# The second mixing's first layer by one level of Strassen's seven products

## The chip, the core and the metric

One core of one Trainium2 chip runs the whole program. The metric is device time in microseconds, the median of the runs shown; the profile is one further execution of the same program. PE is the matrix engine, DVE the vector engine, ACT the scalar engine, POOL the GpSimd engine, SP the engine that issues most DMAs.

## What is computed

```python
def _moe2_ref(x, g_ln, w_ch1, w_ch2):
    mu = np.mean(x, axis=-1, keepdims=True)
    var = np.mean((x - mu) ** 2, axis=-1, keepdims=True)
    xn = (x - mu) / np.sqrt(var + 1e-06) * g_ln
    ch = np.maximum(xn @ w_ch1, 0.0) @ w_ch2
    return x + ch
```

This is the last of three parts. Before it stand a linear attention (8 batches, 8 heads, 576 positions of 64) and a first mixing of tokens and channels (hidden sizes 256 and 1536). The second mixing, above, works on 8 x 576 = 4608 tokens of 512 channels with 2048 hidden channels. The weights arrive as 64-bit floats.

## The kernel before

**Numbers.** Each fp32 operand of a matmul is split into two parts, hi and lo, and each product is three matmuls (`PASSES`, hi-hi, hi-lo, lo-hi). A 64-bit weight is decoded by `decode` (L92): a rescale, three bit operations (L113, L120, L126) and a split (ACT copies hi, POOL subtracts for lo).

**First stage.** `Phase1` (L676) runs nine blocks of 512 tokens. A step is one hidden slice `f` of 128: `L1` (L695; its matmuls L704) makes 12 matmuls of 512 columns into a PSUM tile of the pool `ps_hid`, which has two buffers; ACT and DVE (`relu_split`, L148) turn it into a tile `h`; `L2` (L711; L721) adds 12 matmuls into four accumulators, two steps later (`LAG`). Every block has 12 steps. Beside it run attention and the weight decode, hung into the steps by `later` (so many ticks ahead; a step has four ticks) and by `loads.pump` (so many operations after each layer). `finish` writes the block to DRAM, `y_store` (L651) turns it by four transposes per 128 tokens.

**Second stage.** `Norm` (L802) brings a block back from DRAM and normalises it: DVE subtracts the mean, POOL scales, ACT and DVE split into `xT`. `Phase2` (L850) runs the nine blocks, with 16 steps each. A step is `L1` (L858; matmuls L865; weights `wa2`, moving operand `xT`), the relu and split, and `L2` (L872; matmuls L880; weights `h`, moving operand `wb2`), 12 matmuls of 512 columns each. That makes 9 x 16 x 12 = 1728 matmuls per layer. A `g` stands for two steps: tiles `wa2[g]` and `wb2[g]` lie in the pool `main`, except those of `g` 0 and 1 (steps 0 to 3 of each block), which lie in the pool `w2pool`, further up in SBUF; `xT` and `h` lie in `main`.

**What sets the order.** The program is written out by hand: each engine takes its instructions strictly in the order in which the code issues them, each waiting for semaphores. So an ACT copy that waits for a DMA holds up every ACT instruction behind it. SP's DMAs are issued in order too. The main loop (L999) issues L1, relu and split, decode work, L2 of two steps before, decode work.

**The memories.** PSUM: four accumulators (`ps_acc`), two tiles for L1 (`ps_hid`), two for everything else (`ps_att`). In SBUF the tag `w` of `main` has twelve tiles of 8 KB per partition, for the weights of both stages in turn; the tag `s` has two staging tiles.

## Time and profile before

| | |
|---|---|
| median of 3 runs | 1650.42 us (1649.99 to 1651.19) |
| span of the profiled execution | 1648.4 us, 2.0 us under the median |
| PE busy | 98% of the span |
| DVE, ACT, POOL busy | 40%, 25%, 23% |
| mean granted clock of PE | 0.998 of full speed |
| DMA | 119.71 MB, mean 73 GB/s |

A matmul's duration in the profile is modelled and longer than its slot on the engine, because matmuls are pipelined. The pace is read from start to start: the first of a group of twelve to the first of the next group.

### The profile page before, as it was taken

What the parts mean: (1) busy time and instruction counts of PE and PEld (TensorE: products, weight loads), DVE (VectorE), ACT (ScalarE), POOL (GpSimd) and SP (SyncE); (2) the same over time, 40 slices, a digit from 0 to 9 for tenths busy, and PEclk for the clock granted to TensorE, in tenths of its full rate; (3) what the DMA queues carried; (4) which work ended last, traced back from release to release, by engine and by line L of the source; (5) the groups of instructions that cost most, each with busy time, mean ns of one, the idle gap of its engine ahead of it and who ended that gap; (6) DMA issues with size and microseconds to landing.
All of it is one profiled execution on the core that took longest, in us unless ns stands there. A gap on an engine that the chain in (4) does not pass through costs nothing.

```text
span 1648.4 us, 19985 instructions
## 1 busy us (share of the span) xinstructions
PE 1619.5 (98%) x7954; PEld 1360.3 (83%) x7954; DVE 651.6 (40%) x1265; ACT 407.2 (25%) x819; POOL 379.7 (23%) x349
## 2 busy tenths in 40 slices
PE   5899999999999999999999999999999999999998
PEld 4888888888888888888888888888888888888887
DVE  7876535444343535454478611222212121222211
ACT  5663323323232323322122211111111111111110
POOL 5744612232232424221234310000001010101000
PEclk9999999999999999999999999999999999999999
DMA  8552313122131313134236210100101011111010
GB/s 220 144 168 77 119 37 95 50 54 79 40 95 29 95 43 95 29 102 148 109 96 211 90 58 33 55 35 26 64 26 64 26 35 55 33 58 33 8 43 26
DMA packets 128516, 119.71 MB, mean 73 GB/s; under 512 B 93406, under 2 KB 106534, under 8 KB 123942
## 3 DMA queue, kind: packets, MB, share of 16 engines
q1 hardware_dynamic: 121526, 100.30, 20.4%
q10 hardware_dynamic: 5600, 9.73, 1.6%
q0 software_dynamic: 1296, 8.39, 1.4%
q8 instruction: 63, 1.03, 0.3%
q14 instruction: 31, 0.25, 0.1%
HBM read 86.90 MB, written 31.49 MB: 72 GB/s over the span
## 4 chain that ended last, share of the span: by engine, by line
PE 94%; POOL 2%; DVE 2%; issue 1%; ACT 1%; DMA 0%; SPq 0%; POOLq 0%; ACTq 0%; DVEq 0%
PE ph L865 24%; PE acc L880 24%; PE ph L704 18%; PE acc L721 18%; PE pu L624 4%; PE pg L563 3%; PE pk L533 2%; PE py L654 1%; PE pq L584 1%; PE pq L609 1%; DMA stages<-in_moe_w_tok 0%; POOL w L144 0%; POOL spare L496 0%; POOL yT L745 0%; POOL qn L144 0%
## 5 line engine op out<-in xcount | busy, mean ns | idle before, releaser
L150 DVE SCALAR_TENSOR_TENSOR h<-ph,h 128x512 fp32r<-128x512 f32 x252 | 173.7, 690 | 726.0 <-ACT h L149 725.9
L880 PE MATMUL acc<-w,h 128*128 128x512 f32 x1728 | 418.4, 391 | 0.0
L865 PE MATMUL ph<-xT,w 128*128 128x512 f32 x1728 | 418.2, 391 | 0.0
L865 PEld LDWEIGHTS ph<-xT,w 128*128 128x128 f32 x1728 | 324.6, 188 | 70.3
L880 PEld LDWEIGHTS acc<-w,h 128*128 128x128 f32 x1728 | 324.0, 188 | 70.1
L149 ACT ACTIVATE h<-ph 128x512 fp32r<-128x512 f32 x252 | 150.1, 596 | 776.7 <-PE ph L865 617.0
L704 PE MATMUL ph<-u,w 128*128 128x512 f32 x1296 | 324.7, 395 | 0.0
L721 PE MATMUL acc<-h,w 128*128 128x512 f32 x1296 | 323.6, 394 | 0.0
L721 PEld LDWEIGHTS acc<-h,w 128*128 128x128 f32 x1296 | 237.4, 188 | 47.5
L704 PEld LDWEIGHTS ph<-u,w 128*128 128x128 f32 x1296 | 236.8, 188 | 47.1 <-DVE u L644 0.4
L837 POOL TENSOR_TENSOR yT<-yT,mrb 128x256 f32<-128x256 f32 x72 | 54.7, 789 | 248.1 <-DVE yT L833 248.1
L906 POOL DMA_DIRECT2D out<-y x9 | 5.6, 621 | 346.9 <-DVE y L900 346.9
L481 POOL TENSOR_TENSOR qt<-rawq,qm 128x640 f32<-128x640 f32 x24 | 30.3, 1261 | 228.5 <-PE pt L475 130.5
L135 POOL TENSOR_TENSOR w<-t,w 128x512 fp32r<-128x512 f32 x32 | 41.9, 1311 | 123.2 <-ACT w L134 123.1
L624 PE MATMUL pu<-w,hs 128*128 128x288 f32 x384 | 61.8, 295 | 0.8 <-POOL w L144 0.7
L563 PE MATMUL pg<-w,qn 128*128 128x256 f32 x448 | 58.8, 282 | 2.2 <-POOL qn L144 1.8
L563 PEld LDWEIGHTS pg<-w,qn 128*128 128x128 f32 x448 | 57.0, 189 | 4.6 <-POOL qn L144 2.0
L624 PEld LDWEIGHTS pu<-w,hs 128*128 128x128 f32 x384 | 54.4, 188 | 1.3 <-POOL w L144 1.0
L745 POOL TENSOR_TENSOR yT<-yT,u 128x512 f32<-128x512 f32 x32 | 42.7, 1349 | 37.0 <-issue 31.6
L144 DVE TENSOR_TENSOR qT<-pq,qT 128x512 fp32r<-128x512 f32 (+1 forms) x48 | 22.0, 458 | 71.6 <-ACT qT L142 71.6
L496 POOL TENSOR_TENSOR kt<-rawk,kb 128x640 f32<-128x640 f32 x24 | 38.0, 1583 | 41.4 <-ACT kb L492 41.4
L134 ACT ACTIVATE w<-t 128x512 fp32r<-128x512 f32 x32 | 20.2, 633 | 101.2 <-DVE t L126 100.8
(144 smaller groups left out, 1248.8 us busy)
## 6 DMA issues: line engine op xcount, KB each, us to landing
st<-in_moe_w_ch SPq DMA_DIRECT2D x31, 512.0 KB, 3.8
y_dram<-yn ACTq DMA_DIRECT2D x36, 256.0 KB, 2.4
yT_dram<-yT SPq DMA_DIRECT2D x9, 1024.0 KB, 4.6
yT<-yT_dram SPq DMA_DIRECT2D x9, 1024.0 KB, 4.8
y<-y_dram SPq DMA_DIRECT2D x9, 1024.0 KB, 7.2
vt<-in_v SPq DMA_DIRECT2D x64, 128.0 KB, 2.9
out<-y POOLq DMA_DIRECT2D x7, 1024.0 KB, 4.2
rawk<-in_k SPq DMA_DIRECT2D x54, 128.0 KB, 2.9
```

Source lines behind the costliest of these rows:

```text
L135: nc.gpsimd.tensor_tensor(out=lo, in0=x, in1=hi.bitcast(F32), op=ALU.subtract)
L149: nc.scalar.activation(out=hi, in_=x, func=AF.Relu)
L150: nc.vector.scalar_tensor_tensor(out=lo, in0=x, scalar=0.0, in1=hi.bitcast(F32), op0=ALU.max, op1=ALU.subtract)
L496: nc.gpsimd.tensor_tensor(out=self.kt, in0=self.kr, in1=kb.to_broadcast([P, NC + 1, 2, D]), op=ALU.subtract,)
L563: nc.tensor.matmul(out=pg[:, 0:T], lhsT=self.qn[:, x, c], rhs=w1[:, y, c, :], start=(n == 0), stop=(n == len(terms) - 1),)
L624: nc.tensor.matmul(out=pu[:, 0:HN], lhsT=l, rhs=r, start=(n == 0), stop=(n == len(terms) - 1))
L704: nc.tensor.matmul(out=ps, lhsT=w[:, x, kk, fo:fo + P], rhs=u[:, y, kk], start=(n == 0), stop=(n == 3 * KD - 1),)
L721: nc.tensor.matmul(out=self.acc[dd], lhsT=w[:, x, f % 2, dd * P:(dd + 1) * P], rhs=h[:, y], start=(f == self.f0 and n == 0), stop=(f == se ...
L745: nc.gpsimd.tensor_tensor(out=yT[:, :, x], in0=yT[:, :, x], in1=u[:, 1, :, x].bitcast(F32), op=ALU.add)
L837: nc.gpsimd.tensor_tensor(out=y, in0=y, in1=self.b[:, 1], op=ALU.mult)
L865: nc.tensor.matmul(out=ps, lhsT=w[:, x, kk, fo:fo + P], rhs=xT[:, y, kk], start=(n == 0), stop=(n == 3 * KD - 1),)
L880: nc.tensor.matmul(out=self.acc[c], lhsT=h[:, x, c * P:(c + 1) * P], rhs=w[:, y, f % 2], start=(f == 0 and n == 0), stop=(f == self.f1 - 1 ...
```

## The change

The 512 channels and the 256 hidden channels of a pair of slices are cut into 2 x 2 blocks, the tokens of a block into two halves. Instead of eight block products, seven are made (the variant with 15 additions). Tokens are taken in six blocks of 768 (`NS`), with halves of 384 (`HT`), and hidden channels in eight pairs (`NP`), so a unit `q` is one pair for one block: 48 units.

- **Weights.** `Combine` decodes `w_ch1` in the last two blocks of the first stage, adds four sums on DVE, splits seven combinations (ACT hi, POOL lo) and stores them in DRAM (`wc_dram`, 1.84 MB per pair). None of them stays in SBUF: `ring_load` brings the seven of a unit back from DRAM, two units ahead, into two sets of tiles of `main`.
- **Tokens.** `load_x`, `load_mr`, `hat` (POOL: minus mean, times 1/deviation), `gain` (ACT), four differences `xdiff` (POOL) and seven splits `xsplit` (ACT, DVE) make seven combinations `xc`, which lie in `w2pool`, once per 768 tokens.
- **A unit.** `product(q, i)`, i from 0 to 6: six matmuls of 384 columns each into one of two PSUM banks. `gather(q, i)` adds the products up on ACT and DVE and makes the four `ht` tiles by relu and split. `token_chunk` is the second layer as before: six chunks of 128 tokens, 6 matmuls of 512 columns each, of the unit before, put between the products (`AFTER`).
- **Second-layer weights.** `w2_jobs` decodes pairs 0 to 2 in the last steps of the first stage, pairs 3 to 7 during units 1 to 5. These and `Combine`'s pieces stand in one list, `jobs`, of which seven are taken after each layer of a step (`work(7)`) and two after each product (`work(2)`).
- **The seam.** The last two `L2` of the first stage, its `finish` and four `y_store` are issued inside units 0 and 1. The output goes out by POOL's queue, chunk by chunk.

`Phase2`, `Norm`, `rate` and the old use of `loads` for the second stage are removed.

```diff
--- before.py
+++ after.py
...
+    HT = 3 * P
+    SB = 2 * HT
+    NS = NT // SB
+    NP = NF2 // 2
+    CS = SB // P
+    ORDER = [*range(B - 1), B, B - 1]
+    pos = {j: i for i, j in enumerate(ORDER)}
+    flat = [(j, c) for j in ORDER for c in range(CT)]
...
+    wc_dram = dram.tile([NP, P, 7, 512], F32, name="wc_dram")
...
+        vec, late = nc.vector, t is not None
+        box = {"t": t}
...
+    class Combine:
...
+        def load(self):
+            self.st = []
...
+                st = stage(512)
+                a = w2_ch1[2 * i * P:2 * (i + 1) * P, 4 * self.g * P:4 * (self.g + 1) * P]
+                nc.sync.dma_start(
+                    out=st.rearrange("p (k f) t -> p k (f t)", k=2),
+                    in_=a.rearrange("(k p) f -> p k f", p=P),
+                )
+                self.st.append(st)
...
+            both = [decode(st, None, None, None) for st in self.st]
+            ops = [b[0] for b in both]
+            for b in both:
+                ops += [lambda b=b: [b[n]() for n in (1, 2, 3)], nop, nop]
...
+            ops += [
+                add(1, A21, A22, ALU.add), add(0, "S1", A11, ALU.subtract),
+                add(2, A11, A21, ALU.subtract), add(3, A12, "S2", ALU.subtract),
+            ]
...
+            ops += part(A11, 0) + part(s[:, 0], 1) + part(A12, 2) + [store(0, 3)]
+            ops += part(s[:, 1:3], 3, 2) + [store(3, 2)]
+            ops += part(s[:, 3], 5) + part(A22, 6) + [store(5, 2)]
...
+        def work(n):
+            for _ in range(n):
+                if jobs:
+                    jobs.pop(0)()
...
+            def expand(g):
+
+                d = cs[g].decoding() if g < NP else []
+                f = cs[g - 1].splitting() if g else []
+                ops = []
+                while f or d[:-4]:
+                    ops += f[0:2]
+                    del f[0:2]
+                    if len(d) > 4:
+                        ops.append(d.pop(0))
+                ops += [cs[g + 1].load] if g + 1 < NP else []
+                ops += d
+                if g < NP:
+                    ops.append(lambda: expand(g + 1))
+                jobs[0:0] = ops
...
+                ops = [b[0] for b in both]
+                for b in both:
+                    ops += [lambda b=b: [b[n]() for n in (1, 2, 3)], nop, nop]
+                jobs[0:0] = ops + [b[4] for b in both]
...
+            out = list(made[0][0])
+            for n, (_, go) in enumerate(made):
+                out.append(go)
+                if n + 1 < len(made):
+                    out += made[n + 1][0]
...
+        def ring_load(q, x):
+            n, m = ((0, 4), (4, 3))[x]
+            nc.sync.dma_start(
+                out=ring[q % 2, x].rearrange("p i x k f -> p i (x k f)").bitcast(F32),
+                in_=wc_dram[q % NP, :, n:n + m],
+            )
...
+        def hat(k, th, op):
+            y = xpart(k, th)
+            m = aux(0)[:, op:op + 1].to_broadcast([P, 2, HT])
+            nc.gpsimd.tensor_tensor(
+                out=y, in0=y, in1=m, op=(ALU.subtract, ALU.mult)[op]
+            )
...
+        def xsplit(i, x):
+            nc.scalar.activation(out=xc[i][:, 0], in_=x, func=AF.Copy)
+            nc.vector.tensor_tensor(
+                out=xc[i][:, 1], in0=x, in1=xc[i][:, 0].bitcast(F32), op=ALU.subtract
+            )
...
+                    later(4, lambda: load_x(0))
+                    later(4, lambda: load_mr(0, 0))
+                    for n in range(4):
+                        later(9 + 2 * n, lambda n=n: hat(n % 2, 0, n // 2))
+                    for n in range(4):
+                        later(17 + n // 2, lambda n=n: gain(n, 0))
+                    later(17, lambda: load_mr(0, 1))
+                    for n in range(4):
+                        later(19 + 2 * n, lambda n=n: hat(n % 2, 1, n // 2))
+                    for n in range(4):
+                        later(26 + n // 2, lambda n=n: gain(n, 1))
...
+                    extra[:] = [-1, -1, 0, 1]
+                    later(4, combine_all)
...
+                if f == 6:
+                    ring_tile(1, 0)
+                    ring_tile(1, 1)
+                    later(8, lambda: [ring_load(n, x) for n in range(2) for x in range(2)])
+                if f == 7:
+                    extra[:] = [-1, -1]
+                    jobs += w2_jobs(range(0, 3), lambda i: stage(512))
...
+            loads.pump(7 if now[0] < RUSH else 3)
+            work(7)
...
+        BANK = (0, 1, 0, 1, 0, 1, 0)
...
+        def product(q, i):
+            r = ring[q % 2, 0][:, i] if i < 4 else ring[q % 2, 1][:, i - 4]
+            n, add = 0, i in (2, 6)
+            for kk in range(2):
+                for x, y in PASSES:
+                    nc.tensor.matmul(
+                        out=bank[(BANK[i] + q) % 2][:, 0:HT],
+                        lhsT=r[:, x, kk], rhs=xc[i][:, y, kk],
+                        start=(n == 0 and not add), stop=(n == 5), skip_group_check=add,
+                    )
+                    n += 1
...
+            if i == 0:
+                nc.scalar.activation(out=u2, in_=b(0), func=AF.Copy)
+            elif i == 1:
+                add(u2, u2, b(1))
+            elif i == 2:
+                h = ht["11", q % 2]
+                relu_split(b(0), h[:, 0], h[:, 1])
+            elif i == 3:
+                add(u4, u2, b(1))
+            elif i > 3:
+                add(c, (u4, u4, u2)[i - 4], b((0, 1, 0)[i - 4]))
+                h = ht[("22", "12", "21")[i - 4]]
+                relu_split(c, h[:, 0], h[:, 1])
...
+            p, th, m = q % NP, c // 3, c % 3
+            x0 = ht["11", q % 2] if th == 0 else ht["12"]
+            x1 = ht["21"] if th == 0 else ht["22"]
+            n = 0
+            for f, h in enumerate((x0, x1)):
+                for x, y in PASSES:
+                    nc.tensor.matmul(
+                        out=acc[c],
+                        lhsT=h[:, x, m * P:(m + 1) * P], rhs=wb2[p][:, y, f],
+                        start=(p == 0 and n == 0), stop=(p == NP - 1 and n == 5),
+                    )
+                    n += 1
...
+        ht["11", 0] = main.tile([P, 2, HT], F32R, tag="h", bufs=LAG + 1, name="h11")
+        ht["12"] = w2pool.tile([P, 2, HT], F32R, tag="s3", name="h12")
...
+        at(0, 0, lambda: do_L2(nop))
+        at(0, 1, lambda: do_L2(nop))
+        at(0, 2, last_rows)
...
+            jobs.extend(w2_jobs(range(3, NP), stages, ts))
...
+        for s in range(NS):
+            q0 = s * NP
+            if s + 1 < NS:
+                at(q0 + 1, 3, lambda s=s: load_x(s + 1))
+                at(q0 + 1, 4, lambda s=s: load_mr(s + 1, 0))
+                for n in range(4):
+                    at(q0 + 2, 3 + n, lambda n=n: hat(n % 2, 0, n // 2))
+                for n in range(4):
+                    at(q0 + 3, 1 + n, lambda n=n: gain(n, 0))
+                at(q0 + 3, 0, lambda s=s: load_mr(s + 1, 1))
+                for n in range(4):
+                    at(q0 + 3, 3 + n, lambda n=n: hat(n % 2, 1, n // 2))
...
+                for i in range(7):
+                    at(q0 + 7, i, lambda i=i: split_x(i))
...
+        AFTER = ((3,), (4, 5), (0,), (), (1,), (2,), ())
+        LASTS = ((3,), (4,), (5,), (), (0,), (1,), (2,))
+        for q in range(NQ + 1):
+            for i in range(7):
+                cs = (LASTS if q >= NQ - 1 else AFTER)[i] if q else ()
+                if q < NQ:
+                    product(q, i)
+                for c in cs:
+                    token_chunk(q - 1, c)
+                if q < NQ:
+                    gather(q, i)
+                if (q - 1) % NP == NP - 1:
+                    for c in cs:
+                        finish_chunk((q - 1) // NP, c)
+                for fn in todo.pop((q, i), ()):
+                    fn()
+                if q < NQ - 2 and i in (3, 6):
+                    ring_load(q + 2, i // 4)
...
```

## Rows read from the trace of the kernel before

**Rows 1.** The page: busy time by engine, and the chain that ended last, by engine.

```profile
PE 1619.5 (98%) x7954; PEld 1360.3 (83%) x7954; DVE 651.6 (40%) x1265; ACT 407.2 (25%) x819; POOL 379.7 (23%) x349
...
PE 94%; POOL 2%; DVE 2%; issue 1%; ACT 1%; DMA 0%; SPq 0%; POOLq 0%; ACTq 0%; DVEq 0%
```

**Rows 2.** Groups by form, the second stage's matmuls: busy us, mean ns, idle before.

```profile
L880 PE MATMUL acc<-w,h 128*128 128x512 f32 x1728 | 418.4, 391 | 0.0
L865 PE MATMUL ph<-xT,w 128*128 128x512 f32 x1728 | 418.2, 391 | 0.0
```

**Rows 3.** Timeline of PE in the second stage: start us, us, group.

```profile
846.78 2.96 PE L865 MATMUL ph<-xT,w 128*128 128x512 f32 x12
...
1002.49 2.88 PE L865 MATMUL ph<-xT,w 128*128 128x512 f32 x12
1005.21 2.88 PE L880 MATMUL acc<-w,h 128*128 128x512 f32 x12
...
1024.26 2.96 PE L865 MATMUL ph<-xT,w 128*128 128x512 f32 x12
1027.05 2.92 PE L880 MATMUL acc<-w,h 128*128 128x512 f32 x12
...
1043.73 2.96 PE L880 MATMUL acc<-w,h 128*128 128x512 f32 x12
1046.52 2.90 PE L865 MATMUL ph<-xT,w 128*128 128x512 f32 x12
...
1635.71 8.32 PE L880 MATMUL acc<-w,h 128*128 128x512 f32 x36
```

**Rows 4.** Timeline of PE, shorter matmuls of the attention, two groups in sequence.

```profile
668.12 0.56 PE L624 MATMUL pu<-qT,kvs 128*128 128x288 f32 x3
668.52 0.96 PE L624 MATMUL pu<-w,hs 128*128 128x288 f32 x6
```

**Rows 5.** Timeline, ACT and DVE behind a finished L1.

```profile
1005.41 0.60 ACT L149 ACTIVATE h<-ph 128x512 fp32r<-128x512 f32 x1 [4.17 <-PE ph L865]
...
1006.04 0.69 DVE L150 SCALAR_TENSOR_TENSOR h<-ph,h 128x512 fp32r<-128x512 f32 x1 [4.02 <-ACT h L149]
```

**Rows 6.** Groups by form: decode, split and POOL operations of the first stage.

```profile
L107 ACT ACTIVATE st<-st 128x512 f32<-128x512 f32 x11 | 7.4, 670 | 10.0 <-DMA st<-in_moe_w_tok 5.4 <-DMA st<-in_moe_w_ch 4.0 <-POOL w L144 0.6
L113 DVE TENSOR_SCALAR dt<-st 128x512 uint32<-128x512 uint32 x11 | 7.5, 684 | 0.5 <-ACT st L107 0.5
L144 POOL TENSOR_TENSOR w<-more,w 64x256 fp32r<-64x256 f32 x1 | 0.7, 729 | 0.1
L144 POOL TENSOR_TENSOR w<-st,w 128x512 fp32r<-128x512 f32 x11 | 14.7, 1335 | 18.4 <-ACT w L142 18.4
L481 POOL TENSOR_TENSOR qt<-rawq,qm 128x640 f32<-128x640 f32 x24 | 30.3, 1261 | 228.5 <-PE pt L475 130.5 <-PE pq L584 63.8 <-DVE kmd L477 22.6
```

**Rows 7.** The page's DMA issues: count, KB each, median us to landing.

```profile
st<-in_moe_w_ch SPq DMA_DIRECT2D x31, 512.0 KB, 3.8
...
yT<-yT_dram SPq DMA_DIRECT2D x9, 1024.0 KB, 4.8
y<-y_dram SPq DMA_DIRECT2D x9, 1024.0 KB, 7.2
```

**Rows 8.** Windows: us, busy by engine, granted clock, DMA share, GB/s.

```profile
16.00:30.00 14.00, 8.94 (x51) 7.78 (x51) 13.14 (x29) 7.12 (x15) 11.73 (x11) 0.78 0.95 244
892.00:930.00 38.00, 38.00 (x169) 31.47 (x168) 32.57 (x49) 9.24 (x16) 18.38 (x16) 1.00 0.50 171
```

**Rows 9.** Source view, splitting of xT: duration ns min/median/max.

```profile
L844 ACT ACTIVATE xT<-yT,gT x36: 708/715/727, 828.8 to 1532.3; 128x512 fp32r<-128x512 f32 x36
L845 DVE SCALAR_TENSOR_TENSOR xT<-yT,gT,xT x36: 736/752/1652, 832.7 to 1533.1; 128x512 fp32r<-128x512 f32 x36
```

**Rows 10.** Timeline, the end of the kernel.

```profile
1642.03 2.73 DVE L900 TENSOR_TENSOR y<-acc,y 128x512 f32<-128x512 f32 x4 [4.80 <-PE acc L880]
1642.75 2.37 SPq L903 DMA_DIRECT2D out<-y  x4
```

More of the change, by code (lines that the diff above doesn't have):

```diff
@@ L657, in y_store @@
             )
[L658 to L661 removed]
+        if j == B:
+            yn = yn_t[j][:, c * DM:(c + 1) * DM]
         else:
@@ new lines, in w2_job, with load, fn, go @@
+        def w2_job(g, stages, ts=None):
+            box = {}
+            def load(i):
+                def fn():
+                    if i == 0:
+                        wb2[g] = main.tile([P, 2, 2, DM], F32R, tag="w", bufs=NF1, name="w")
+                    st = box[i] = stages(i)
+                    f0 = (2 * g + i) * P
+                    nc.sync.dma_start(
+                        out=st.rearrange("p d t -> p (d t)"), in_=w2_ch2[f0:f0 + P, :]
+                    )
+                return fn
+            def go():
+                both = [
+                    decode(box[i], lambda x: x, wb2[g][:, 0, i], wb2[g][:, 1, i], ts and ts[i])
+                    for i in range(2)
+                ]
+                if ts:
+                    jobs[0:0] = [x for pair in zip(*both) for x in pair]
+                    return
+                ops = [b[0] for b in both]
+                for b in both:
+                    ops += [lambda b=b: [b[n]() for n in (1, 2, 3)], nop, nop]
+                jobs[0:0] = ops + [b[4] for b in both]
+            return [load(0), load(1)], go
@@ new lines, in w2_jobs, with ring_tile @@
+        def w2_jobs(gs, stages, ts=None):
+            made = [w2_job(g, stages, ts) for g in gs]
+            out = list(made[0][0])
[3 more added lines that the diff above has]
+                    out += made[n + 1][0]
+            return out
+        ring = {}
+        xc, xs = [], []
+        def ring_tile(i, x):
+            m = 4 if x == 0 else 3
+            ring[i, x] = main.tile([P, m, 2, 2, P], F32R, tag="w", bufs=NF1, name="wr")
@@ L1047 @@
                 do_L2()
-                loads.pump(rate(4, 3, 4))
+                loads.pump(4)
+                work(7)
                 tick()
-        while pend:
-            do_L2()
+        while jobs:
+            work(1)
+        while ticks:
+            tick()
+        NQ = NS * NP
+        BANK = (0, 1, 0, 1, 0, 1, 0)
+        XOF = ("P1", "P6", "P2", "P5", "P7", "P3", "P4")
+        bank = [ps_hid.tile([P, 512], F32, tag="h", name="pp") for _ in range(2)]
+        acc, ht, tmp = {}, {}, {}
@@ new lines, in load_y @@
+        def load_y(s):
+            for j, c, k, n in runs(s * CS, CS):
+                nc.sync.dma_start(
+                    out=y_tile(k, n).rearrange("p (c d) -> p c d", d=DM), in_=y_dram[j][:, c:c + n]
+                )
+        yb = []
+        sd = main.tile([P, 1024], F32, tag="s", bufs=2, name="sd")
+        tmp["t3"] = sd[:, 0:2 * HT].rearrange("p (k n) -> p k n", k=2)
+        tmp["u"] = main.tile([P, 1024], F32, tag="s", bufs=2, name="su")
+        tmp["c"] = [main.tile([P, 512], F32, tag="t", bufs=2, name="sc") for _ in range(2)]
@@ new lines @@
+        AFTER = ((3,), (4, 5), (0,), (), (1,), (2,), ())
[16 more added lines that the diff above has]
+                    ring_load(q + 2, i // 4)
+                if q and jobs:
+                    work(2)
```

405 lines of the change are left out of this document (235 added, 170 removed).

## The prediction

> **What bounds the kernel now.** I read the page first: PE is busy for 98% of the span, and the chain that ended last runs on PE for 94% [rows 1]. The groups by form come next: both layers of the second stage count 1728 matmuls of 512 columns with no idle time before them [rows 2]. So the second stage is bound by how many slots of PE it needs, and a slot is to be measured, because the mean of 391 ns is modelled. In the timeline twelve matmuls take 1005.21 - 1002.49 = 2.72 us, so a slot is 226.7 ns [rows 3]. At 2.4 GHz 512 columns are 213.3 ns; 13.3 ns come on top. The stretch from the first L865 to the end of the last L880 is 1644.03 - 846.78 = 797.25 us [rows 3].
>
> Not all steps are that fast. At the start of each block, twelve take 1027.05 - 1024.26 = 2.79 us in L1 and 1046.52 - 1043.73 = 2.79 in L2 [rows 3]: 232.5 ns. These are the steps 0 to 3, whose weights lie in w2pool while the other operand lies in main. So I read it as a matter of where the two operands lie: 6 ns more where one is in each pool. DMA isn't the reason: the windows show a stretch at 171 GB/s [rows 8] that has no slower matmuls than a quiet one.
>
> **What the change takes from PE.** L1: a unit had 2 x 4 x 3 matmuls of 768 columns, now 7 x 6 = 42 matmuls of 384; 48 units give 2016. No row shows 384 columns. The nearest rows are 288 columns, (668.52 - 668.12) / 3 = 133 ns [rows 4], and 512, 226.7 or 232.5 ns [rows 3]. On a straight line 384 columns take 173 ns with the fast end and 176 with the slow one; 173 + 6 = 179 is the upper bound. The new moving operand xc lies in w2pool and its weights in main, so the slow end applies: I take 176. L1 is 2016 x 0.176 = 354.8 us.
>
> L2: 1728 x 0.2267 = 391.7. One of the four ht tiles lies in w2pool, a quarter of the weights: 432 x 0.006 = 2.6. Sum 394.3. The stretch further holds, as before, 24 leftover L2 matmuls of the first stage (5.4) and 16 transposes (2.0). Together 756.5, against 797.25: **40.7 us less** on PE (bounds 33.9 at 179 ns, 46.7 at 173).
>
> **What is added, and what covers it.**
>
> A unit, steady: PE needs 42 x 0.176 + 36 x 0.227 = 15.6 us. Behind a finished L1 the last matmul starts at 1002.49 + 11 x 0.2267 = 1004.98, ACT at 1005.41 and DVE at 1006.04 [rows 5]. So a gather's add, relu and split take about 0.27 + 0.53 + 0.58 + 0.6 = 2.0 us after PE has gone on (512-element durations scaled to 384, estimates). A bank is written again one product and a chunk later, 1.06 + 1.36 = 2.4 us, and needs only the add or the split from PSUM, at most 1.4 us. The chunk that reads the last two ht tiles comes 3.5 us after the product. So a unit costs nothing extra by its chain; the cover is 1.0 to 1.4 us. If DVE is over 1 us late there, PE pays each time.
>
> The weights' stream: 1.84 MB per 15.6 us is 118 GB/s, beside some 45 of the rest; the window with 171 GB/s has a DMA share of 0.50 [rows 8], so some 340 would be full. A ring_load is issued 1.4 units, 22 us, before its use. Nothing.
>
> POOL beside DVE: per 768 tokens eight hats and four differences. 640 elements take 1.26 us [rows 6], so about 1.5 and 1.9 us each, 15 bursts over five blocks. DVE's split of two SBUF tiles is 0.752 at the median and up to 1.652 beside POOL [rows 9]. Most of that stays under the cover; I take 2 us (0 to 10).
>
> Unit 0 has no chunks between its products, so its gathers lie bare: product 5 waits for gather 3, which stands on DVE behind four adds of 0.68 [rows 10]. Product 4 waits 0.4, product 5 some 2.0 us: 2.5.
>
> The output's last chunk goes by POOL instead of SP; the adds end as before [rows 10]: 0.5 (0 to 2).
>
> **Combine, in the last two blocks.** A pair has 29 jobs, 14 are taken per step of 5.44 us, so a slot is 11.3 us. The chain that must fit: load of two chunks (3.8 alone [rows 7], then 1.6 for the second's bytes, and about 2 behind the stores just issued), two rescales of 0.67, the copies and POOL's six subtractions (five of 0.73, one of 1.34 [rows 6]), and only then the next load to the same staging tiles. That is about 12 us: ACT falls behind 0.8 us per pair, 6 us at the end. The relu in its queue can be late by 6.6 us: after an L1 ends, its PSUM tile is wanted three layers, 8.2 us, later, and relu and split end 1.5 us after it [rows 5]. I take 1.5 us (0 to 20).
>
> **The seam is the dear part.** In steps 7 to 9 of the last block stand the decodes of pairs 0 to 2: 39 jobs in three steps of 5.44. But each pair's loads wait for POOL to leave the two staging tiles, and the ACT rescale that waits for the load stands ahead of the relu of the next step. Counted from the end of L1 of step 7: load_mr waits for POOL's fourth hat (0.8), the first loads land at 6 and 7.6, ACT reaches the relu of step 8 at 14. POOL frees the tiles at 11.2 and 14.4, so pair 1's first load lands at 15. Between it and the second one the four ring loads are issued, 3.67 MB, 11 us at 340 GB/s. If a queue's transfers land in order, the second one lands at 27; the rescale, three DVE operations of 0.68 [rows 6], two gains and two copies follow, and step 9's split ends near 33, where PE wants it at 21. Step 8's costs 2.4, step 9's 11.5, and pair 2 repeats it for step 10, 4.6: 18.5 us. If the second load needn't wait for the ring, it lands at 18.5 and the sum is 10. The same megabyte takes 4.8 us in one place and 7.2 in another [rows 7], which speaks for order. After such a pause the clock may fall: in 16 to 30 us, with PE idle in between, 0.78 of full was granted [rows 8], some 3 us lost. I take 15 us for all of it (0 to 25).
>
> **Sum.** 1.5 + 15 + 2.5 + 2 + 0.5 = 21.5 added, 40.7 saved: 19.2 less. On the profiled span that is 1648.4 - 19.2 = 1629.2; the median of the runs lies 2.0 above the span, so **1631.2**.
>
> **Two rules set beside rows.** The rows give a slot of 13.3 ns over the columns' time, and L1 saves some 37 us by it. The Trainium skill, "TensorE: Matmul & The Clock Gate", section "Back-to-back issue gap", gives a matmul alone its columns at 2.4 GHz plus 2.5 ns. By that the 288 more matmuls would hardly cost, L1 would save 1728 x 215.8 - 2016 x 162.5 = 45.3 us, and the sum would be 1623; here the trace differs with 226.7.
>
> The split of xT shows that DVE and POOL hinder one another [rows 9]. The Trainium skill, "SBUF — State Buffer", section "SBUF: two separate sides", says that a DVE operation with two SBUF inputs and a GpSimd operation exclude one another for the whole instruction; the median of 0.752 shows that it is rare here, the maximum that it happens.
>
> **The rivals.**
> - **Staging hidden.** If the first loads come earlier than I count (POOL less behind), ACT is never late by over 6.6 us at the seam. Then 15 and 1.5 go: 1614.7. For it: SP, waiting for nothing, runs far ahead; against it: the ring loads stand in the midst of the pair's loads. 0.22.
> - **Each burst of POOL holds the splits fully.** With three splits held 1.5 us each, the chunk that reads the last tile comes 0.7 us late, in 15 units: 10 us on top, 1641. For it the maximum of 1.652, against it the median [rows 9]. 0.10.
> - **Slower: Combine's chain paces PE.** Its place is ACT's rescale behind the load. If loads land in 10 us instead of 7 behind the stores, and POOL is slowed, the chain is 18 us against the slot of 11.3. From some 14 us per pair on it eats the whole gain, as 8 x (14 - 11.3) - 6.6 = 15 joins the 21.5 above; at 18 it is 8 x 6.7 - 6.6 = 47, so 1650.4 - 40.7 + 20 + 47 = 1677. 0.15.
> - **The scheme saves nothing:** 384 columns cost a slot of 512, 2016 x 0.2267 = 457 for L1, 102 more than reckoned: 1733. The 288 columns at 133 ns speak plainly against it. 0.03.
>
> The forecast's own case, 1622 to 1641, has 0.50.
>
> **How the numbers follow.** A measurement can tell 0.2%, 3.3 us, from no change. Faster is nearly all of the first two cases and the third, 0.80; same, 0.06, lies where Combine's chain is near 14 us; slower, 0.14, is the rest. The range takes the hidden seam with fast matmuls, 1610, and reaches into Combine's case, 1658.
>
> **What would show it.** In the changed trace: 42 matmuls of 384 columns at 176 ns from start to start; PE idle of 10 us or more in the last block of the first stage, ended by DVE's or ACT's work on h, with ACT waiting for a DMA into the staging tiles; ring loads that land two units early; no idle time of PE in units 6 and later. Wrong it would be with PE idle in every unit, ended by DVE, or with a pace of 384 columns above 180 ns.

## The result, and the profile after

The changed kernel takes **1666.91 us** (1665.21 to 1667.54), the kernel before in the same runs 1650.20 us. The ratio is 1.0099, 95% interval 1.0085 to 1.0113: **slower by 1.0%**, where 1631.2 us was forecast, in a range from 1610 to 1658. The profiled execution has a span of 1664.6 us.

The page of the changed kernel, with the engines' busy time and then the chain that ended last (lines answering to [rows 1]):

```profile
PE 1599.8 (96%) x8241; PEld 1401.3 (84%) x8241; DVE 794.7 (48%) x1551; ACT 494.6 (30%) x1022; POOL 495.7 (30%) x412
...
PE 43%; DMA 2%; DVE 1%; issue 0%; ACT 0%; SPq 0%; POOL 0%; POOLq 0%; DVEq 0%; ACTq 0%
PE pp L1213 20%; PE acc L1251 15%; PE acca L1251 8%; DMA yb<-in_moe_w_ch 2%; DVE sc L1226 0%; DVE h L156 0%; DVE r L786 0%; ACT h L155 0%; DVE su L1226 0%; PE py L659 0%; DVE yb L126 0%; DVE r L785 0%; DVE r L784 0%; DVE yT L745 0%; POOL out L1272 0%
```

PE is busy for 19.7 us less than before, and yet the span is 16.2 us longer: PE now stands idle. The chain of waits doesn't run to the front any more, because it ends in a DMA into yb, a staging load of the second stage's weights.

The timeline of PE shows the second stage, from the first product (L1213, 384 columns) over one steady unit to the last token matmuls (L1251, 512 columns); it answers to [rows 3]:

```profile
877.68 1.47 PE L1213 MATMUL pp<-xc,wr 128*128 128x384 f32 x6 [2.32 <-DVE h L156]
...
1150.96 1.21 PE L1213 MATMUL pp<-xc,wr 128*128 128x384 f32 x6
1152.01 2.95 PE L1251 MATMUL acc<-w,h 128*128 128x512 f32 x12
1154.80 1.21 PE L1213 MATMUL pp<-xc,wr 128*128 128x384 f32 x6
...
1166.62 1.22 PE L1213 MATMUL pp<-xc,wr 128*128 128x384 f32 x6
...
1655.60 2.88 PE L1251 MATMUL acca<-w,h 128*128 128x512 f32 x12
```

Six products take 1152.01 - 1150.96 = 1.05 us, 175 ns each (176 was forecast). A unit takes 1166.62 - 1150.96 = 15.66 us (forecast: 756.5 - 7.4 over 48 units, 15.61). Over 48 units that is 2.6 us more than reckoned, so the scheme saves 38.1 us, not 40.7. With 42 products at 175 ns, (15.66 - 7.35) / 36 = 231 ns are left for a token matmul, against 228 in the sum. The saving is there.

So 16.2 + 38.1 = **54.3 us were added, where 21.5 were forecast**. Three stretches hold them. The stage begins at 877.68 instead of 846.78 [rows 3], 30.9 us late. It lasts 1658.48 - 877.68 = 780.8 us, which is 21.7 more than 797.25 - 38.1. The tail behind the last matmul is 1.7 us longer. The windows say where PE didn't work (us, busy by engine, granted clock of PE, DMA share, GB/s):

```profile
730.00:845.00 115.00, 106.24 (x465) 86.71 (x464) 65.86 (x121) 45.03 (x95) 57.99 (x61) 0.96 0.73 268
...
846.00:866.00 20.00, 10.32 (x45) 7.88 (x43) 8.45 (x12) 6.26 (x12) 8.81 (x6) 0.89 0.60 236
866.00:885.00 19.00, 15.05 (x52) 12.20 (x53) 13.23 (x15) 8.70 (x14) 11.88 (x7) 0.76 0.16 56
885.00:970.00 85.00, 72.00 (x340) 63.60 (x339) 49.05 (x87) 19.04 (x38) 28.44 (x18) 0.92 0.54 189
...
877.68:976.14 98.46, 85.46 (x395) 75.55 (x395) 58.01 (x97) 23.68 (x47) 31.76 (x21) 0.91 0.52 181
976.14:1658.48 682.34, 682.34 (x3391) 613.99 (x3390) 282.18 (x468) 149.86 (x285) 121.83 (x93) 1.00 0.45 153
```

The last two windows cut the stage at 976.14, where unit 5 starts its products: from there on PE is never idle, and all that the stage has too much lies in units 0 to 4. Before 976 there are three places: **Combine** (730 to 845), the **seam** (846 to 885) and **units 1 to 5** (885 to 970; named after the decode of pairs 3 to 7, which is issued in units 1 to 5; the stretch itself runs from within unit 0 to within unit 4). In each one the clock is below full too, 0.76 to 0.96. Behind a pause stand stretches at 0.50, the lower level of 1.2 GHz. PE's timeline has one after the longest pause in Combine:

```profile
805.12 5.46 PE L724 MATMUL acc<-h,w 128*128 128x512 f32 x12 [4.58 <-DVE yT L745]
810.37 1.58 PE L707 MATMUL ph<-u,w 128*128 128x512 f32 x6
```

Twelve matmuls take 810.37 - 805.12 = 5.25 us there, instead of 2.72 [rows 3]; a window from 804 to 810 grants 0.50. What PE waited for, from 700 us on (us in total, times, longest):

```profile
PE ph L707 <- DVE h L156: 11.3, 2, 9.9
PE pp L1213 <- DVE h L156: 8.0, 3, 5.2
PE pp L1213 <- DVE su L1226: 5.2, 2, 3.6
PE acc L724 <- DVE yT L745: 4.6, 1, 4.6
PE py L659 <- ACT yn L667: 2.6, 1, 2.6
PE pp L1213 <- DVE sc L1226: 2.0, 1, 2.0
PE pm L794 <- DVE mr L789: 1.6, 1, 1.6
```

PE is 35.3 us idle, always for VectorE or ScalarE. What the clock lacks in the first four windows above (115 x 0.04 + 20 x 0.11 + 19 x 0.24 + 85 x 0.08) is some 18 us, an estimate, and rather too much, since a low clock costs nothing while PE is idle. The two together come to 53.5 us, beside 54.3 - 1.7 = 52.6 that were added ahead of the tail.

VectorE and ScalarE waited for something else. Two lists of waits name it: ScalarE's in Combine (735 to 840), where L113 is the rescale of freshly loaded weights,

```profile
ACT stage L113 <- DMA stage<-in_moe_w_ch: 21.2, 6, 7.9
ACT st L113 <- DMA st<-in_moe_w_ch: 16.7, 6, 5.2
```

and VectorE's in units 1 to 5 (885 to 970), where L111 is the same rescale on VectorE:

```profile
DVE yb L111 <- DMA yb<-in_moe_w_ch: 16.3, 7, 7.4
```

In the seam the timeline of SP's queue shows the order of the loads (L1028: a chunk of a weight pair; L1067: the ring loads):

```profile
847.60 0.33 SPq L1028 DMA_DIRECT2D st<-in_moe_w_ch  x1
848.02 1.82 SPq L1067 DMA_DIRECT2D wr<-wc_dram  x4
850.51 0.34 SPq L1028 DMA_DIRECT2D st<-in_moe_w_ch  x1
```

The view of the tile st from 846 to 866 gives the times from issue to landing, with the 512 KB chunk behind the four ring loads as the longest:

```profile
DMA to landing us min/median/max: 3.5/7.4/11.2
```

**Theory.** In all three places a load into a staging buffer is issued when its buffer has just come free, and the first operation on it stands next in the in-order queue of ScalarE or VectorE, ahead of the relu, split or finish that PE needs. Where the load takes longer than the engine has other work, PE stops, and it then pays again at the lower clock. **Rivals:** the added operations themselves are too many, or hold one another up (VectorE and GpSimd); or the transfers don't fit through the DMA engines, whatever their order.

### The profile page after: what moved, and what is told of

Its sections match the earlier page's. It is cut to its first block, busy times and chain, and to the rows that moved or that the text cites. A ratio compares the mean times of both kernels' runs of the same rounds, so it can differ in the third digit from the quotient of the medians.

```text
span 1664.6 us, 21709 instructions
## 1 busy us (share of the span) xinstructions
PE 1599.8 (96%) x8241; PEld 1401.3 (84%) x8241; DVE 794.7 (48%) x1551; ACT 494.6 (30%) x1022; POOL 495.7 (30%) x412
## 3 DMA queue, kind: packets, MB, share of 16 engines
q1 hardware_dynamic: 145750, 202.02, 37.9%
## 5 line engine op out<-in xcount | busy, mean ns | idle before, releaser
L1213 PE MATMUL pp<-xc,wr 128*128 128x384 f32 x2016 | 398.2, 340 | 15.3 <-DVE h L156 8.0
L1213 PEld LDWEIGHTS pp<-xc,wr 128*128 128x128 f32 x2016 | 362.6, 189 | 36.5 <-DVE h L156 9.5
L707 PE MATMUL ph<-u,w 128*128 128x512 f32 x1296 | 327.3, 398 | 11.3 <-DVE h L156 11.3
L1251 PE MATMUL acc<-w,h 128*128 128x512 f32 x1152 | 289.8, 393 | 0.0
L724 PEld LDWEIGHTS acc<-h,w 128*128 128x128 f32 x1296 | 240.9, 191 | 53.5 <-ACT wc L886 5.0
L1251 PEld LDWEIGHTS acc<-w,h 128*128 128x128 f32 x1152 | 214.4, 188 | 38.8
L1251 PE MATMUL acca<-w,h 128*128 128x512 f32 x576 | 148.3, 394 | 0.0
L156 DVE SCALAR_TENSOR_TENSOR h<-ph,h 128x512 fp32r<-128x512 f32 x108 | 74.0, 686 | 144.8 <-ACT h L155 144.5
L156 DVE SCALAR_TENSOR_TENSOR h<-sc,h 128x384 fp32r<-128x384 f32 x144 | 90.1, 626 | 94.3 <-ACT h L155 94.3
L1098 POOL TENSOR_TENSOR xs<-xs 128x768 f32<-128x768 f32 x48 | 89.4, 1887 | 144.8 <-DMA xs<-mr_dram 144.8
L1251 PEld LDWEIGHTS acca<-w,h 128*128 128x128 f32 x576 | 107.8, 189 | 16.7
L155 ACT ACTIVATE h<-ph 128x512 fp32r<-128x512 f32 x108 | 64.2, 594 | 142.3 <-PE ph L707 140.9
L156 DVE SCALAR_TENSOR_TENSOR h<-pp,h 128x384 fp32r<-128x384 f32 x48 | 26.7, 556 | 144.1 <-ACT h L155 144.1
```

Of the source, the lines that this page charges most:

```text
L155: nc.scalar.activation(out=hi, in_=x, func=AF.Relu)
L156: nc.vector.scalar_tensor_tensor(out=lo, in0=x, scalar=0.0, in1=hi.bitcast(F32), op0=ALU.max, op1=ALU.subtract)
L707: nc.tensor.matmul(out=ps, lhsT=w[:, x, kk, fo:fo + P], rhs=u[:, y, kk], start=(n == 0), stop=(n == 3 * KD - 1),)
L724: nc.tensor.matmul(out=self.acc[dd], lhsT=w[:, x, f % 2, dd * P:(dd + 1) * P], rhs=h[:, y], start=(f == self.f0 and n == 0), stop=(f == se ...
L1098: nc.gpsimd.tensor_tensor(out=y, in0=y, in1=m, op=(ALU.subtract, ALU.mult)[op])
L1213: nc.tensor.matmul(out=bank[(BANK[i] + q) % 2][:, 0:HT], lhsT=r[:, x, kk], rhs=xc[i][:, y, kk], start=(n == 0 and not add), stop=(n == 5), ...
```

## The experiments

All times are medians of at least four executions; the changed kernel's 1666.91 is what an experiment's gain is counted from, unless another is named.

| kernel | us | ratio to before, 95% interval |
|---|---|---|
| changed kernel | 1666.91 | 1.0099 (1.0085 to 1.0113) |
| e1_units: pairs 3 to 7 loaded ahead | 1657.52 | 1.0040 (1.0025 to 1.0055) |
| e2_ring: ring loads earlier | 1664.14 | 1.0082 (1.0067 to 1.0097) |
| e3_combine: staging freed earlier | 1653.61 | 1.0018 (1.0008 to 1.0028) |
| e5_pad: 128 bytes of padding | 1662.90 | 1.0074 (1.0059 to 1.0089) |
| e6_order: ring loads behind pairs 1 and 2 | 1659.88 | 1.0051 (1.0034 to 1.0068) |
| e7_seam: e3 and the seam loaded ahead | 1640.37 | 0.9943 (0.9928 to 0.9958) |
| e8_all: e7 and e1 | 1631.26 | 0.9885 (0.9870 to 0.9900) |
| e9_all_pad: e8 and the padding | 1629.06 | 0.9871 (0.9857 to 0.9886) |
| e10_stride: e8 with the old stride of h | 1630.22 | 0.9877 (0.9862 to 0.9891) |
| e11_stride_pad: e10 and the padding | 1630.73 | 0.9882 (0.9866 to 0.9899) |

**Units 1 to 5: e1_units.** The pairs' chunks become one stream in which each load is issued three chunks ahead.

```diff
-            jobs.extend(w2_jobs(range(3, NP), stages, ts))
...
+            def chunk(n):
+                ops = go(n)
+                if n + 3 < len(chunks):
+                    ops.append(lambda: load(n + 3))
+                if n + 1 < len(chunks):
+                    ops.append(lambda: chunk(n + 1))
+                jobs[0:0] = ops
+
+            jobs.extend([lambda n=n: load(n) for n in range(3)] + [lambda: chunk(0)])
```

> Edit: the weight pairs 3 to 7 of the second layer (units 1 to 5 of the first group) are loaded chunk by chunk, each load three chunks ahead of its decode, in place of two chunks loaded right ahead of theirs; same operations, same bytes. Theory (a staging load with nothing between it and its use holds up VectorE's queue, and TensorE behind it): the changed kernel waits 12.1 us on VectorE and loses about 3.3 us more at the granted clock of 0.5 after those waits in units 1 to 5, so the time falls by 10 to 15 us, to 1652 to 1657, and the waits of the products on L156 and L1226 (15.2 us in that list) fall under 4 us. Rival one (VectorE and GpSimd lock each other out, whatever the order of the loads): the same operations run in the same units, so under 3 us come back. Rival two (the queue cannot carry ring, tokens and weights together): the loads still land too late and under 5 us come back.

9.4 us came back, just under the 10 expected. In the list of VectorE's waits from 885 to 970 the one for the load is gone:

```profile
DVE yb L111 <- DMA yb<-in_moe_w_ch: 0.3, 1, 0.3
```

The products' waits for VectorE fell from 15.2 to 6.1 us, not under 4:

```profile
PE pp L1213 <- DVE h L156: 2.4, 1, 2.4
...
PE pp L1213 <- DVE sc L1226: 2.2, 2, 1.9
PE pp L1213 <- DVE su L1226: 1.5, 1, 1.5
```

The bytes are the same, and the loads are no quicker: the trace has the landing of five of the first six, and four of these take 8.5 to 11.4 us beside the ring loads, the fifth 5.3. VectorE no longer waits for them, so bandwidth isn't the limit there. Part of the rest belongs to the first rival. VectorE's timeline has two operations of 2.22 us that elsewhere take 0.69 and 0.56:

```profile
925.08 2.22 DVE L132 SCALAR_TENSOR_TENSOR yb<-yb 128x512 uint32<-128x512 uint32 x1
...
930.55 2.22 DVE L156 SCALAR_TENSOR_TENSOR h<-sc,h 128x384 fp32r<-128x384 f32 x1 [0.65 <-ACT h L155]
```

and GpSimd's has its hats at just those times:

```profile
924.58 4.44 POOL L1098 TENSOR_TENSOR xs<-xs 128x768 f32<-128x768 f32 x2 [5.01 <-DMA xs<-mr_dram]
...
930.54 3.91 POOL L1098 TENSOR_TENSOR xs<-xs 128x768 f32<-128x768 f32 x2
```

The Trainium skill, "SBUF — State Buffer", section "SBUF: two separate sides", says that a VectorE operation with two SBUF inputs and a GpSimd operation exclude each other for a whole instruction; these rows agree, with 1.5 and 1.7 us more than elsewhere. That is some 3 us on VectorE here, where the loads were worth 9 us of the whole time. How much of the 3 us reached PE was not tried alone.

**The seam, a first attempt: e2_ring.** The ring loads go ahead instead of between.

```diff
                 if f == 4:
                     ring_tile(0, 0)
                     ring_tile(0, 1)
+                    later(5, lambda: [ring_load(0, x) for x in range(2)])
                 if f == 6:
...
-                    later(8, lambda: [ring_load(n, x) for n in range(2) for x in range(2)])
+                    later(1, lambda: [ring_load(1, x) for x in range(2)])
```

> Edit: the four first loads of the combined weights (3.67 MB) are issued some ten microseconds earlier, so that they no longer stand between the two chunk loads of weight pair 1. Theory (transfers of one queue land in their order, so a 512 KB load behind 3.67 MB comes 11 us later): the wait of the first layer at 857.3 us (10.1 us) falls to 2 to 5 us and with its stretch of half clock behind it 6 to 10 us come back: 1657 to 1661. Rival (the seam is paced by the operations of VectorE, ScalarE and GpSimd themselves, not by the load): the wait stays within 2 us and the time is the same within 2 us.

A miss: 2.8 us came back, which the two intervals don't tell from nothing, and the long wait, 9.9 us before, is still 9.2. That the wait stayed within 2 us was the rival's sign. But SP's queue shows another reason: two of the four ring loads had gone at 821.79, the other two came behind SP's earlier entries and stood right ahead of pair 0:

```profile
836.42 0.94 SPq L1067 DMA_DIRECT2D wr<-wc_dram  x2
837.45 1.53 SPq L1028 DMA_DIRECT2D st<-in_moe_w_ch  x2
```

Both chunks of pair 0 landed some 11 us later (median of the issues from 836 to 839):

```profile
st<-in_moe_w_ch SPq DMA_DIRECT2D x2, 512.0 KB, 11.0
```

So the stall moved from pair 1 to pair 0. Pair 1, with nothing ahead, landed in 3.5 us. This speaks for order in the queue: the same 512 KB take 3.5 us alone and 11 behind ring loads, at two different places. The Trainium skill, "DMA: Bandwidth & Descriptors", section "Queues, rings and completion order", says that each DMA engine takes the descriptors of a ring in their order; the trace agrees, with 11.2 us in the changed kernel and 11.0 here. The bytes ahead alone don't give the time, though: here two ring loads of 1.84 MB stood right ahead, in the changed kernel four of 3.67 MB, and what else was on its way was not separated.

**The seam, the other way: e6_order.** Ring loads behind the loads of pair 1 and of pair 2.

```diff
-                    later(8, lambda: [ring_load(n, x) for n in range(2) for x in range(2)])
...
-                    jobs += w2_jobs(range(0, 3), lambda i: stage(512))
+                    seam = w2_jobs(range(0, 3), lambda i: stage(512))
+                    for m, n in ((5, 0), (9, 1)):
+                        seam.insert(m, lambda n=n: [ring_load(n, x) for x in range(2)])
+                    jobs += seam
```

> Edit: of the changed kernel, only the place of the four ring loads in SP's queue: two of them (1.84 MB) behind the second load of weight pair 1, two behind the loads of pair 2. In the run that issued them earlier the 10 us stall moved from pair 1's load to pair 0's: the loads of pair 0, issued 1 us behind 1.84 MB of ring loads, landed 10.7 and 11.4 us later, and those of pairs 1 and 2, with nothing ahead, 3.5 to 4.3 us later. Theory (order of landing): with nothing large ahead of pair 0 and 1 the load takes 3.5 to 4.5 us, the longest wait of the first layer in the seam falls from 9.9 to under 5 us, and the time falls by 4 to 9 us against the changed kernel, to 1658 to 1663. Rival (two staging buffers with load, decode and split in series, about 10 us a pair, are the bound by themselves): under 2 us come back, and the waits only spread over the three pairs.

7.0 us came back at the median, as the theory has it. The four executions lie far apart, 1656.61 to 1664.21, and the one with the trace is the slowest of them, only 2.2 us under the changed kernel's. In it the first layer's longest wait fell to 3.1 us, but a wait of 6.1 us now stands at the first units:

```profile
PE pp L1216 <- DVE h L156: 12.2, 4, 6.1
...
PE ph L707 <- DVE h L156: 4.0, 2, 3.1
```

The order of landing shows here from the other side. Pair 1's second chunk was issued at 852.7, the two ring loads behind it from 853.10 on, and it landed in 3.7 us with their 1.84 MB on the way at the same time (the issues from 848 to 854):

```profile
st<-in_moe_w_ch SPq DMA_DIRECT2D x2, 512.0 KB, 3.7
```

So in this load the place in the queue counted, not that the ring loads shared the DMA engines. SP's queue shows the loads of pair 0 from 839.10 on and those of pair 2 only from 860.12 on:

```profile
839.10 13.91 SPq L1028 DMA_DIRECT2D st<-in_moe_w_ch  x4
...
860.12 1.74 SPq L1028 DMA_DIRECT2D st<-in_moe_w_ch  x2
```

Two pairs in 21 us: with two staging buffers, load, decode and split run one after the other, about 10 us a pair. So the rival is borne out for the rest of the seam, and the theory for the part that moved.

**Combine: e3_combine.** The blocks read from staging are split first, and the next load follows them at once.

```diff
-            ops += part(A11, 0) + part(s[:, 0], 1) + part(A12, 2) + [store(0, 3)]
-            ops += part(s[:, 1:3], 3, 2) + [store(3, 2)]
-            ops += part(s[:, 3], 5) + part(A22, 6) + [store(5, 2)]
+            ops += part(A11, 0) + part(A12, 2) + part(A22, 6)
+            ops += part(s[:, 0], 1) + [store(0, 3)]
+            ops += part(s[:, 1:3], 3, 2) + [store(3, 2)]
+            ops += part(s[:, 3], 5) + [store(5, 2)]
...
+                if f and g + 1 < NP:
+                    f.insert(6, cs[g + 1].load)
...
```

> Edit: in Combine the three blocks that are split straight from the staging buffers (A11, A12, A22) are split first, and the next pair's load is issued right behind them instead of after the four sums; the operations are the same. Theory (the loop load, decode, split is a few tenths longer than its slot, about 11.5 us against 11.3, so ScalarE ends up waiting for the load 5 us at a time, and the block's finish is late behind it): the load starts about 3 us earlier, the waits on L667, L789 and L745 (8.8 us in the list of waits) fall under 3 us, and with 3 to 4 us of half clock after them 8 to 12 us come back: 1655 to 1659. Rival (the extra operations themselves are too many for VectorE and ScalarE in those two blocks, or the loads share the queue with the 2 MB of u): under 3 us come back.

13.3 us came back, more than expected. The window of the two blocks with the same work, 463 matmuls, is 102 us long instead of 115, with PE busy throughout and the clock at full, and with more bytes per second than before (300 against 268 GB/s):

```profile
730.00:832.00 102.00, 101.50 (x463) 83.69 (x462) 70.06 (x117) 42.13 (x89) 55.62 (x58) 1.00 0.81 300
```

Of ScalarE's waits for staging loads, 37.9 us in the changed kernel, this is left (725 to 830):

```profile
ACT st L113 <- DMA st<-in_moe_w_ch: 1.4, 2, 1.1
```

Neither the number of operations nor the bandwidth was the limit. The three idle waits that vanished come to 8.8 us; the other 4.5 us fit the matmuls at half clock behind them, which no list of waits shows (0.04 of the clock over 115 us is 4.6 us, an estimate).

**The seam with loads ahead: e7_seam,** on top of e3. Three staging buffers; the first three chunks are loaded as soon as Combine leaves them; a chunk per step of PE. With `PACE` = 4 the decode is also spread over the last six steps of the block.

```diff
+        def seam_chunk(n):
+            g, i = n // 2, n % 2
+            def go():
+                if i == 0:
+                    wb2[g] = main.tile([P, 2, 2, DM], F32R, tag="w", bufs=NF1, name="w")
+                ops = decode(seam_st[n], lambda x: x, wb2[g][:, 0, i], wb2[g][:, 1, i])
+                if n + 3 < 6:
+                    ops.append(lambda: seam_load(n + 3))
+                jobs[0:0] = ops
+            return go
...
-                    later(8, lambda: [ring_load(n, x) for n in range(2) for x in range(2)])
+                    later(12, lambda: [ring_load(0, x) for x in range(2)])
+                    later(18, lambda: [ring_load(1, x) for x in range(2)])
+                    jobs += [seam_chunk(0), seam_chunk(1)]
...
-            work(7)
+            work(PACE if o.j == B and f > 5 else 7)
...
```

> Edit: on top of the reordered Combine (1653.6 us), pairs 0 to 2 are decoded in the seam chunk by chunk with three staging buffers, each load three chunks ahead of its decode, the first three issued as soon as Combine has freed their buffers; the ring loads stand behind the last of them; the same operations spread over the last six steps of block 8. Theory (loads without prefetch): the seam's two long waits (12.9 us on L156 in the reordered run) fall under 3 us, and with the half clock behind them 11 to 15 us come back: 1639 to 1643. Rival (VectorE, ScalarE and GpSimd have too much to do in the seam): at 20.6 us of VectorE and 20.6 us of GpSimd in 35 us they would still stop TensorE, and under 5 us come back.

13.2 us came back against e3. The first layer waits 0.9 us in the seam, where e3 had 12.9; it is the same decoding with the same engines. So it isn't that they have too much to do in all. How much is owed to the earlier loads, and how much to the spreading, which leaves fewer operations to a step, was not separated.

```profile
PE ph L707 <- DVE h L156: 0.9, 1, 0.9
```

**All together: e8_all,** e7 with the stream of e1, whose first three loads don't wait for a turn:

```diff
-            jobs.extend([lambda n=n: load(n) for n in range(3)] + [lambda: chunk(0)])
+            for n in range(3):
+                load(n)
+            jobs.append(lambda: chunk(0))
```

> Edit: all three together: reordered Combine, seam with prefetch, pairs 3 to 7 with prefetch (its first three loads issued at once when the buffer comes free). Theory (the three places add up, since each is a stall of its own on TensorE's path): 1666.9 - 13.3 - 9.4 - 11 to 15 = 1629 to 1633, faster than the kernel before by about 1 per cent, which is what the prediction gave for the change without them. Rival (a saved stall comes back in the next place): over 1640.

1631.26 us, in the middle of what was expected. In all 13.3 + 13.2 + 9.1 = 35.6 us came back, and the kernel is 1.15% faster than the kernel before. The sum comes out by itself, since each step is measured from the one before; that the places add up shows in e1's stream, which gave 9.4 us alone and 9.1 on top of the others. PE's waits from 690 us on:

```profile
PE pp L1247 <- DVE h L156: 3.5, 2, 2.4
PE pp L1247 <- DVE sc L1260: 2.7, 2, 2.1
PE pp L1247 <- DVE su L1260: 1.5, 1, 1.5
PE ph L707 <- DVE h L156: 0.9, 1, 0.9
```

PE's timeline, first product and last token matmuls:

```profile
850.66 1.35 PE L1247 MATMUL pp<-xc,wr 128*128 128x384 f32 x6 [2.38 <-DVE h L156]
...
1619.81 2.88 PE L1285 MATMUL acca<-w,h 128*128 128x512 f32 x12
```

The stage begins 3.9 us later than in the kernel before and lasts 1622.69 - 850.66 = 772.0 us, 25.2 less. Units 0 to 4 take 89.71 us of it, where the changed kernel took 98.46; the rest is the same, 682.3 us in both:

```profile
850.66:940.37 89.71, 83.69 (x394) 72.71 (x395) 61.72 (x98) 24.83 (x49) 35.29 (x22) 0.94 0.70 214
```

**The pace: e5_pad, e9_all_pad, e10_stride, e11_stride_pad.** The token matmuls are 3 ns slower than reckoned. I looked for it in where the operands lie, first with

```diff
+                    w2pool.tile([P, 32], F32, name="pad")
```

> Edit: 128 unused bytes per partition at the head of the second pool, nothing else. In the changed kernel a matmul of 512 columns starts every 226.7 us/1000 behind another when both its operands lie in the same pool, and about 233 ns when they lie in different pools; the tiles of the two pools stand 128 bytes apart modulo 512. Theory A (the alignment decides): with the pad the products take 173 ns in place of 175 and the token matmuls with h12 227 in place of 233, in all 4 to 8 us: 1659 to 1663. Theory B (what decides is which part of the memory the two operands lie in, or something else): no change within 1.5 us.

> Edit: the version with all three, and 128 unused bytes at the head of the second pool. If the pad's 4 us are an effect of addresses alone (products 173 ns in place of 175 ns, 2016 of them, token matmuls the same within 1 ns), it takes 2 to 5 us off the version without it; if they were the scatter of the runs, nothing within 1.5 us.

4.0 us with the changed kernel, where the two intervals overlap, and 2.2 us with e8. The products went from 175 to 173 ns at the median. The token matmuls didn't improve, 231 ns on the mean as before: they changed from one fixed pattern of 224 to 240 ns to another of 224 to 236, also in chunks whose operands both lie in the pool that had not moved. Then the distance of the low parts in h:

```diff
-        ht["11", 0] = main.tile([P, 2, HT], F32R, tag="h", bufs=LAG + 1, name="h11")
+        ht["11", 0] = main.tile([P, 2, 512], F32R, tag="h", bufs=LAG + 1, name="h11")[:, :, 0:HT]
...
```

> Edit: on the version with all three, the five tiles of h keep the low parts 2048 bytes behind the high parts, as the kernel before does, instead of 1536; nothing else. Question: why a token matmul starts 231 ns after the one before it where the forecast had the 226.7 and 232.7 ns of the kernel before (228.2 on the mean). In the trace of this version the same matmul takes a fixed pace by where its operands lie: 227 ns for some pairs of w tile and h slice, 231 to 240 for others. Theory A (where the slices of h lie decides): with the old stride the mean falls towards 227 to 228 ns; 1728 matmuls by 2.5 to 4 ns is 4 to 7 us, to 1624 to 1627. Theory B (384 columns in place of 512 before the switch, or the distance between the two pools, decides): within 1.5 us of 1631.3.

> Edit: the same, with the 128 bytes at the head of the second pool as well. Theory A: the pad takes 1 to 2 ns off a product (2 us) as it did before, so 2 us under the version with the stride alone. If the two edits move the same operands against each other, the pad gives nothing or takes back up to 3 us.

Theory A failed: 1630.22 us, and the token matmuls keep their paces within 1 ns at the median, though half of the slices have moved by 512 bytes. With the pad on top it is 1630.73, so the time shows no gain there. The steady units settle what the pad does. In the changed kernel unit 16's second product starts at 1150.96 and the one 28 units later at 1589.79, 15.67 us per unit; with the pad these are 1150.38 and 1588.36, 15.64. e8 and e10 have 15.67 as well, e9 and e11 15.64. Over 48 units this is 1.4 us, every time. The rest of the 4.0 and 2.2 us lies ahead of the steady units, and there e11 lost what it had gained: its first product starts 1.6 us later than e10's. What sets the pace of a token matmul between 224 and 240 ns stays open; 1728 matmuls at 231 instead of 228 ns are some 5 us in this kernel.

## Why the prediction was wrong

By its own steps:

- **What the change takes from PE: right in mechanism, 2.6 us too much.** 384 columns take 175 ns (176 forecast), and the whole unit 15.66 us (15.61). The rival that 384 columns cost a slot of 512 is refuted. The token matmuls took 231 ns against 228. (The lower bound given there, 33.9 us at 179 ns, should be 40.7 - 2016 x 0.003 = 34.7.)
- **A unit costs nothing extra by its chain, the weights' stream nothing: right** for units 5 on, 682 us of 682 busy. **POOL beside DVE, 2 us:** in the steady units none of it reached PE, though the split's longest is 1.69 us there where its median is 0.56:

```profile
L156 DVE SCALAR_TENSOR_TENSOR h<-sc,h x125: 557/558/1694, 942.3 to 1599.6; 128x384 fp32r<-128x384 f32 x125
```

(the source view of L156 in the changed kernel, 940 to 1600: duration ns min/median/max). A hat took 1.89 us where 1.5 was reckoned. What the meetings in the early units cost PE was not tried alone.
- **Combine, "I take 1.5 us": wrong by an order.** The chain was rightly found longer than its slot, 12 us against 11.3. Its size was already off on paper: the durations listed there, the copies not counted, add up to 3.8 + 1.6 + 2 + 2 x 0.67 + 5 x 0.73 + 1.34 = 13.7 us. From the load at 739.13 to the one at 805.29 the five pairs took 13.2 us each, PE's stalls included. By the rule that the prediction used for its rival, 8 x (13.7 - 11.3) - 6.6, that would have been 12.6 us. (By the same sum the gain is eaten at 14.7 us per pair, not at some 14.) And the delay was thought to be lost only at the end, and to be covered by the 6.6 us for the relu alone. ScalarE's and VectorE's queues also hold the transposes' copies, the norm's roots and the finish of the block, which have less cover: L667, L789 and L745 are the three waits. e3 removed 13.3 us with no operation less. The rival of that name had the right place, at 13.3 us rather than 47.
- **The seam, "I take 15 us": right,** mechanism and size. The stage's start is 30.9 us late; without Combine's 13.3 that leaves 17.6. The second chunk landed 11.2 us behind the ring loads (11 forecast), and e2 and e6 show that its place in the queue does it. The 17.6 are a difference, not measured alone, and made up otherwise than reckoned: the first layer waited 11.3 us where 18.5 were counted, the first product 2.3, and the clock of 0.83 from 846.78 to 877.68 gives the rest. That 15, taken between two sums, came so near is in part luck.
- **The step that failed most is one that isn't there.** The decode of pairs 3 to 7 in units 1 to 5 was priced nowhere: "a unit costs nothing extra" was worked out for a steady unit, and "no idle time of PE in units 6 and later" leaves the first ones out. There VectorE waited 16.3 us for staging loads, and the stage grew by 21.7 us beyond the pace. Unit 0's 2.5 us and the 2 for POOL lie within that. e1 took 9.4 back, e1's loads on top of e7 9.1. So the late loads are shown for some 9 of the 21.7 us. The other 12.9, which e8 still has, stay open: all PE waits there are for VectorE's additions and splits, VectorE itself waits only 1.4 us for a load, and the clock is 0.94. That is what the first rival says, that the added operations are too many or hold one another up, and no run tried it alone. Unit 0, with 2.5 us forecast, has its share in it: 19.10 us long in the changed kernel and 18.90 in e8, where its matmuls and transposes come to some 13.8 by their paces.
- **The tail, 0.5:** measured 1.7.

Sum: 13 and 18 us instead of 16.5 for Combine and seam, 21.7 instead of 4.5 for the early units, 1.7 instead of 0.5 for the tail, 54 against 21.5. Signs set down beforehand came true (384 columns at 175 ns, 11.3 us of idle PE in the last block, no idle time from unit 6 on), but none of them looked at Combine or at the first units, where the forecast failed. With the same scheme and the loads ahead, e8 lands at 1631.26, beside the 1631.2 forecast; that is a coincidence in part, since its 18.5 us of added time are made up differently: 3.9 at the start, 12.9 in the stage, 1.7 in the tail. The rival with the staging hidden gave 1614.7; e8 comes no nearer, because the first units still cost 12.9 us.

## What to carry to other kernels

Where decoded weights are streamed, price each load by what stands ahead of it in its own queue, and each wait for it by all that stands behind it in the waiting engine's queue; loads issued earlier, with the same operations partly reordered and spread, turned a loss of 1.0% into a gain of 1.2%. A cost worked out for the steady unit says nothing about the first units, where the set-up work is: list them one by one. And a load that is moved forward may only hit the next user: look at what it then stands in front of.

## What the runs showed that was not expected

- A stall of PE costs more than its idle time. In Combine 8.8 us of waits were worth 13.3 us. The granted clock (0.96 over 115 us, 1.00 over the same work without the waits, and 0.50 right behind a pause) points to the rest; the list of waits doesn't show it.
- 512 KB took 3.5 us from issue to landing with an empty queue, 3.7 us with 1.84 MB behind it, and 11.0 to 11.2 us with 1.84 to 3.67 MB right ahead, in the same queue.
- Matmuls of one shape run at fixed paces between 224 and 240 ns, by their place in the unit, in nearly the same pattern in every steady unit; 128 bytes in another pool changed the pattern, 512 bytes in one operand did not.
